# Channel attention followed by a top-128 expert layer: pass 1 of a batch and pass 2 of the batch before it, interleaved chunk by chunk

## The chip, the cores and the metric

The kernel runs on one core of a Trainium2 chip. The metric is the device time of one execution in microseconds (us): 358.91 us is the median of three runs (358.47 to 360.29). The core has a matrix engine (PE, which loads weights on PEld), a vector engine (DVE), a scalar engine (ACT), GpSimd (POOL), and SyncE (SP). In this kernel POOL issues all loads and SP all plain stores; 16 DMA engines move them. Each engine's instructions stand in the order in which the program wrote them, and wait on semaphores where an input is not there yet.

## The reference

For each of B = 4 batches, q, k, v are 6208 x 256 (float32):

```
s = kn.T @ qn / tau            # 256 x 256; qn, kn: columns divided by their norm over N
a = softmax(s, last axis)
x = v @ a                      # 6208 x 256
scores = x @ w_gate            # 6208
top = the 128 rows of x with the highest scores
out = x;  out[top] += sigmoid(scores[top]) * (relu(x[top] @ w1) @ w2)
```

So no row of `x` can be formed before all of q and k of its batch have been read (pass 1), and the expert layer of a batch can't choose its 128 rows before all its scores are there (after pass 2).

## The kernel before, in words

N is cut into six chunks of 1024 rows (8 rows to a partition) and a rest of 64. A chunk of q, k or v is one load by POOL that casts float32 to bf16: 1 MiB read, 512 KiB written to SBUF, a *tile* in what follows. The list `units` fixes the load order, and `pump` issues from it as long as the next entry has a free buffer (five chunk pairs of q and k, six chunks of v). `consumed(u)` frees the buffer of a unit at the place in the program where it was last used, and pumps; so the loads stand on POOL in that order, among the gathers and scatters.

- **Pass 1** (`p1_steps`, L187 to L191): per chunk eight steps of six matmuls, which add k.T q to `s_ps` and the Gram blocks (whose diagonals are the squared norms) to `g_ps`.
- **Softmax** (`softmax_a`, `softmax_b`, `softmax_c`, L204 to L264): mostly small DVE operations in a chain, one matmul (L233) that spreads a row of factors over the partitions, two exponentials on ACT. It leaves `a_sb` and, for the scores, `aw_sb` = a @ w_gate.
- **Pass 2** (`p2_groups`): a group is four rows to a partition, so a chunk has two. Eight PE transposes of v (L283), a DVE copy (L286), then for each row the output matmul (L309) and the score matmul (L312), both with the same transposed v as weights; ACT copies the output to a stage tile (L316), and SP stores a chunk of 1 MiB.
- **Expert layer** (`moe_stages`, a generator): seven rounds of counting (`cmp`, `cnt`, then a matmul at L367 that adds the counts over the partitions) close in on the score threshold; then the 128 row numbers (L414), a gather of their v rows (`vg`, POOL, L416), x again for these rows (L423 to L434), the two dense layers (L456, L464), and a scatter (POOL, L471). Each `yield` ends a stage. `slot()` lets the oldest generator run one stage; it is called between pieces of the passes, so a stage's instructions stand between those pieces on PE and DVE.

Before, the driver ran, for each batch, all of pass 1 with a slot at every second step, then the softmax, then all of pass 2; the expert layer of a batch ran in the slots of the next batch's pass 1, and that of the last batch by itself at the end:

```python
units = [(kind, b, ci) for b in range(B) for kind in ("qk", "v") for ci in range(NFULL + 1)]
...
for b in range(B):
    run_p1(b)
    ...
    run_p2(b)
    side.append(moe_stages(b))
```

The stores of batch 2 from chunk 1 on were held back (`deferred`) until the last but one load of all.

Of the kernel before, what the change touches and what calls it, by code (L numbers as in the profile page):

```python
# [9 lines left out]
F32 = mybir.dt.float32  # L10
# [16 lines left out]
def kernel(  # L27
# [30 lines left out]
    ST_BUFS = 12  # L58
# [5 lines left out]
    vt_pool = ctx.enter_context(tc.tile_pool(name="vt_pool", bufs=3))  # L64
# [24 lines left out]
    units = [(kind, b, ci) for b in range(B) for kind in ("qk", "v") for ci in range(NFULL + 1)]  # L89
# [65 lines left out]
    nc.vector.memset(wrow[:, NCOL - 1:NCOL], 0.0)  # L155
    ones_col = const.tile([P, NCOL], BF16)
# [15 lines left out]
    def p1_steps(b, ci):  # L172

        if ci == 0:
            acc[b] = (ps_s.tile([P, 2, C], F32, name="s_ps"), ps_g.tile([P, 4, P], F32, name="g_ps"))
# [23 lines left out]
    def softmax_a(b):  # L199
        s_ps, g_ps = acc[b]  # L200
        junk = smx.tile([P, P], F32, name="junk")
# [28 lines left out]
        for cc in range(2):  # L230
            nc.vector.tensor_scalar_mul(diag[:, cc, :], ident_f, rn[:, cc:cc + 1])
        rq_ps = ps_m.tile([P, 512], F32, name="m_ps")
        nc.tensor.matmul(rq_ps[:, 0:C], lhsT=ones_f, rhs=diag.rearrange("p a c -> p (a c)"),  # L233
                         start=True, stop=True)
        return rn, rq_ps

    def softmax_b(b, rn, rq_ps):
        s_ps, g_ps = acc[b]
# [4 lines left out]
        for cc in range(2):  # L243
            ss = smx.tile([P, C], F32, name=f"ss{cc}")
            nc.vector.scalar_tensor_tensor(out=ss, in0=s_ps[:, cc, :], scalar=rn[:, 2 + cc:3 + cc],  # L245
                                           in1=rq, op0=ALU.mult, op1=ALU.mult)
            nc.scalar.activation(e[:, cc, :], ss, AF.Exp, accum_out=rsum[:, cc:cc + 1])  # L247
        return e, rsum

    def softmax_c(b, e, rsum):  # L250
# [19 lines left out]
    deferred = []  # L270

# [17 lines left out]
    def p2_matmul(b, g, vt_sb):  # L289
        ci, s0, n = g  # L290
        parts = P if ci < NFULL else REM
        a_sb, aw_sb = a_tiles[b]
        if ci == 0 and s0 == 0:
            sc_tiles[b] = ps_sc.tile([P, NCOL, 2], F32, name="sc_ps")
        sc_ps = sc_tiles[b]
        if s0 == 0:
# [5 lines left out]
        for pair in range((n + 1) // 2):  # L302
            o_ps = ps_o.tile([P, 2, C], F32, name="o_ps")
            m = min(2, n - pair * 2)
            for pj in range(m):
                j = pair * 2 + pj
                col = ci * RPP + s0 + j
                for cc in range(2):
# [3 lines left out]
                    nc.tensor.matmul(sc_ps[:parts, col, :], lhsT=vt_sb[:, cc, j, :parts],  # L312
                                     rhs=aw_sb[:, cc, :],
                                     start=cc == 0 and col in (0, NCOL - 1),
                                     stop=cc == 1 and col >= NCOL - 2)
# [9 lines left out]
    def moe_stages(b):  # L325
# [8 lines left out]
        nc.vector.tensor_reduce(out=mx, in_=sc, axis=AX.X, op=ALU.max)  # L334
        yield
        mps = ps_m.tile([P, 512], F32, name="m_ps")
        nc.tensor.transpose(mps[0:1, 0:P], in_=mx, identity=ident_f)

        lohi = moe.tile([1, 2], F32, name="lohi")
        top = moe.tile([1, 1], F32, name="top")  # L340
        nc.vector.tensor_reduce(out=lohi[:, 0:1], in_=mps[0:1, 0:P], axis=AX.X, op=ALU.min)
        nc.vector.tensor_reduce(out=top, in_=mps[0:1, 0:P], axis=AX.X, op=ALU.max)
        nc.vector.tensor_tensor(out=lohi[:, 1:2], in0=top, in1=lohi[:, 0:1], op=ALU.subtract)
        yield
        mps = ps_m.tile([P, 512], F32, name="m_ps")
        nc.tensor.matmul(mps[:, 0:2], lhsT=ones_f[0:1, :], rhs=lohi, start=True, stop=True)
        steps = moe.tile([P, NSTEP], F32, name="steps")
        lo = moe.tile([P, NSTEP + 1], F32, name="lo")
        nc.vector.scalar_tensor_tensor(out=lo[:, 0:1], in0=mps[:, 1:2], scalar=-1e-6, in1=iota_col,
                                       op0=ALU.mult, op1=ALU.bypass)  # L350
        nc.vector.tensor_tensor(out=lo[:, 0:1], in0=mps[:, 0:1], in1=lo[:, 0:1], op=ALU.add)
        for i in range(NSTEP):
            nc.vector.tensor_scalar(out=steps[:, i:i + 1], in0=mps[:, 1:2],
                                    scalar1=1.00001 / (NTHR + 1) ** (i + 1), scalar2=None, op0=ALU.mult)
        for i in range(NSTEP):
# [113 lines left out]
        while deferred and b == B - 2:  # L469
            yield  # L470
# [105 lines left out]
```

## Time and profile before

| | |
|---|---|
| median of three runs | 358.91 us (358.47 to 360.29) |
| the profiled execution's own time | 358.95 us |
| its span, first to last instruction | 357.2 us |
| busy: PE, DVE, ACT, POOL | 220.6, 143.9, 65.8, 56.2 us |
| mean granted TensorE clock | 0.794 of 2.4 GHz |
| DMA: loads (queue q0), stores (queue q1) | 39.98 MB and 25.56 MB, as written |

The 1.75 us between span and time lie outside the instructions. The granted clock is that of PE: 1.0 means 2.4 GHz and 0.5 means 1.2 GHz. Loads count by the bf16 bytes that they write, half of what they read.

### The profile page before, as it was taken

The numbers are of one execution on the slowest core, as the hardware profiler recorded it, in microseconds if no ns is written. First come the engines' busy times: TensorE is split into PE (matmuls) and PEld (weight loads), VectorE is DVE, ScalarE is ACT, GpSimd is POOL, SyncE is SP. The second block draws the span as 40 slices with busy tenths as digits, with TensorE's granted clock in tenths as the row PEclk, the third lists the DMA queues.
The fourth block names the chain that finished last, engine by engine and source line by source line (L and its number), as shares of the span: only waits on it lengthen the run. The fifth ranks groups of instructions, "written<-read, shape, count | busy, mean of one in ns | idle before, by whom it ended". The sixth has DMA issues, their size and how long they took to land.

```text
span 357.2 us, 6052 instructions
## 1 busy us (share of the span) xinstructions
PE 220.6 (62%) x2528; PEld 189.5 (53%) x2528; DVE 143.9 (40%) x543; ACT 65.8 (18%) x129; POOL 56.2 (16%) x103
## 2 busy tenths in 40 slices
PE   0986546995670483898672854997686639930050
PEld 0775434984460382697562753896575628920030
DVE  0000054437820126444880246345862363458520
ACT  1000003660000011474000101671000115720010
POOL 7222322003132030000603030003310010000100
PEclk9999675999785595699888695799788957985555
DMA  7999999999999989187999967201998802850000
GB/s 133 213 213 210 212 212 213 277 317 314 291 213 212 212 155 206 64 345 309 178 214 210 215 135 144 119 2 26 212 213 290 347 15 117 352 246 0 2 6 15
DMA packets 17354, 65.91 MB, mean 185 GB/s; under 512 B 1968, under 2 KB 4656, under 8 KB 14256
## 3 DMA queue, kind: packets, MB, share of 16 engines
q0 software_dynamic: 13408, 39.98, 57.1%
q1 hardware_dynamic: 3920, 25.56, 17.4%
q8 instruction: 19, 0.31, 0.3%
q14 instruction: 7, 0.06, 0.0%
HBM read 79.04 MB, written 25.95 MB: 294 GB/s over the span
## 4 chain that ended last, share of the span: by engine, by line
issue 39%; DMA 29%; PE 19%; DVE 8%; POOL 2%; POOLq 0%; ACT 0%; ACTq 0%
DMA k_ch<-in_k_dram 13%; DMA v_ch<-in_v_dram 7%; PE s_ps L187 5%; DMA q_ch<-in_q_dram 5%; DMA vg<-in_v_dram,idx 4%; PE o_ps L309 4%; PE g_ps L191 3%; PE g_ps L189 3%; PE vt_ps L283 2%; DVE cmp L360 1%; DVE cnt L364 1%; POOL q_ch L105 1%; DVE junk L204 1%; DVE thr L357 1%; PE m_ps L233 1%
## 5 line engine op out<-in xcount | busy, mean ns | idle before, releaser
L187 PE MATMUL s_ps<-q_ch,k_ch 128*128 128x256 bf16 x384 | 103.4, 304 | 19.1 <-DMA k_ch<-in_k_dram 19.1
L189 PE MATMUL g_ps<-q_ch 128*128 128x128 bf16 x384 | 92.0, 240 | 0.0
L191 PE MATMUL g_ps<-k_ch 128*128 128x128 bf16 x384 | 91.7, 239 | 0.0
L309 PE MATMUL o_ps<-a_sb,vt_sb 128*128 128x256 bf16 x392 | 67.2, 287 | 10.8 <-DVE a_sb L258 10.2
L187 PEld LDWEIGHTS <-k_ch 128*128 128x128 bf16 x384 | 41.6, 108 | 38.2 <-DMA k_ch<-in_k_dram 19.6
L312 PE MATMUL sc_ps<-aw_sb,vt_sb 128*128 128x2 bf16 x392 | 58.6, 171 | 4.8 <-DVE aw_sb L264 4.8
L316 ACT COPY stage<-o_ps 128x512 f32<-128x512 f32 x96 | 54.3, 586 | 36.9 <-PE o_ps L309 36.8
L286 DVE COPY vt_sb<-vt_ps 128x1024 bf16<-128x1024 bf16 (+1 forms) x52 | 34.0, 655 | 55.6 <-PE vt_ps L283 55.6
L309 PEld LDWEIGHTS <-vt_sb 128*128 128x128 bf16 x392 | 40.9, 104 | 22.1 <-DVE a_sb L258 8.5
L191 PEld LDWEIGHTS <-k_ch 128*128 128x128 bf16 x384 | 42.0, 109 | 8.8
L189 PEld LDWEIGHTS <-q_ch 128*128 128x128 bf16 x384 | 41.5, 108 | 0.3
L312 PEld LDWEIGHTS <-vt_sb 128*128 128x128 bf16 x392 | 38.5, 98 | 2.9 <-issue 2.5
L283 PE MATMUL vt_ps<-ident_b,v_ch 128*128 128x128 bf16 x384 | 34.1, 244 | 0.0
L105 POOL DMA_DIRECT2D q_ch<-in_q_dram x24 | 13.4, 560 | 108.6 <-PE g_ps L191 96.5
L283 PEld LDWEIGHTS <-v_ch 128*128 128x128 bf16 x384 | 27.4, 111 | 2.3 <-issue 1.1
L446 ACT ACTIVATE gate<-ssc 128x1 f32<-128x1 f32 x4 | 0.8, 203 | 147.0 <-DVE ssc L443 147.0
L367 PE MATMUL m_ps<-cnt,ones_b 128*128 128x8 bf16 x28 | 4.7, 168 | 34.0 <-DVE cnt L364 34.0
L204 DVE CUSTOM_DVE_ANT_0 junk<-g_ps,ident_f 128x128 f32<-128x128 f32 x16 | 4.7, 291 | 49.7 <-PE g_ps L191 49.3
L423 PE MATMUL vt_ps<-ident_b,vg 128*128 128x128 bf16 x8 | 1.5, 282 | 32.9 <-DMA vg<-in_v_dram,idx 32.9
L247 ACT ACTIVATE e<-ss 128x256 f32<-128x256 f32 x8 | 3.3, 408 | 92.6 <-DVE ss L245 92.6
L423 PEld LDWEIGHTS <-vg 128*128 128x128 bf16 x8 | 0.5, 108 | 33.5 <-DMA vg<-in_v_dram,idx 33.5
L105 POOL DMA_DIRECT2D v_ch<-in_v_dram x24 | 13.0, 560 | 31.5 <-DMA k_ch<-in_k_dram 14.1
(116 smaller groups left out, 202.6 us busy)
## 6 DMA issues: line engine op xcount, KB each, us to landing
out_dram<-stage SPq DMA_DIRECT2D x24, 1024.0 KB, 5.6
q_ch<-in_q_dram POOLq DMA_DIRECT2D x24, 512.0 KB, 15.2
k_ch<-in_k_dram POOLq DMA_DIRECT2D x24, 512.0 KB, 15.4
v_ch<-in_v_dram POOLq DMA_DIRECT2D x24, 512.0 KB, 14.8
w_sb<-in_moe_w_dram POOLq DMA_DIRECT2D x2, 512.0 KB, 20.1
out_dram<-stage_rem SPq DMA_DIRECT2D x4, 64.0 KB, 8.3
wg_bcast<-in_moe_w_gate_dram SPq DMA_DIRECT2D x1, 128.0 KB, 3.8
q_rem<-in_q_dram POOLq DMA_DIRECT2D x4, 32.0 KB, 12.0
```

Of the source, the lines that this page charges most:

```text
L105: ins = nc.gpsimd.dma_start(out=t, in_=view(src, b, ci))
L187: nc.tensor.matmul(s_ps[:, cc, :], lhsT=ks[:, sl], rhs=qs, start=first and cc == 0, stop=last and cc == 1)
L189: nc.tensor.matmul(g_ps[:, cc, :], lhsT=qs[:, sl], rhs=qs[:, sl], start=first and cc == 0, stop=False)
L191: nc.tensor.matmul(g_ps[:, 2 + cc, :], lhsT=ks[:, sl], rhs=ks[:, sl], start=False, stop=last and cc == 1)
L204: nc.vector.tensor_tensor_reduce(out=junk, in0=g_ps[:, i, :], in1=ident_f, scale=1.0, scalar=0.0, op0=ALU.mult, op1=ALU.add, accum_out=nsq ...
L233: nc.tensor.matmul(rq_ps[:, 0:C], lhsT=ones_f, rhs=diag.rearrange("p a c -> p (a c)"), start=True, stop=True)
L283: nc.tensor.transpose(vt_ps[:, cc, j, :parts], in_=vt[:parts, s0 + j, cc * P:(cc + 1) * P], identity=ident_b[:parts, :parts])
L286: nc.vector.tensor_copy(vt_sb[:, :, :n, :parts], vt_ps[:, :, :n, :parts])
L309: nc.tensor.matmul(o_ps[:parts, pj, :], lhsT=vt_sb[:, cc, j, :parts], rhs=a_sb[:, cc, :], start=pj == 0 and cc == 0, stop=pj == m - 1 and ...
L312: nc.tensor.matmul(sc_ps[:parts, col, :], lhsT=vt_sb[:, cc, j, :parts], rhs=aw_sb[:, cc, :], start=cc == 0 and col in (0, NCOL - 1), stop= ...
L316: nc.scalar.copy(st[:parts, s0 + pair * 2:s0 + pair * 2 + m, :], o_ps[:parts, :m, :])
L367: nc.tensor.matmul(mps[:, 0:NTHR], lhsT=ones_b, rhs=cnt, start=True, stop=True)
```

## The change

- Load order and program order are now those of `phase(b)`: after the first chunk of q and k of batch b, two chunks of v of batch b-1 follow each chunk pair of q and k, until v is used up. Pass 2 of batch b-1 so runs between the chunks of pass 1 of batch b. There are B+1 phases; the last has v of the last batch alone.
- The softmax becomes a generator in three stages; it copies `s_ps` to SBUF first, so that the next pass 1 can take the PSUM bank. Slots come after each half chunk of pass 1 and each group of pass 2.
- Transposes of v are written two pieces ahead of their group.
- In the last batch, pass 2 first does only the scores (`p2_score`) for all groups, and keeps the 13 transposed groups (14 `vt` buffers in place of 3); then `moe_stages` of that batch starts, with one group of output matmuls (`p2_out`) after each of its stages.
- Held stores: batch 2 from chunk 2 on, behind the load of chunk 4 of the last v. Stage buffers go from 12 to 9.
- In the threshold search the range is found with one matmul in place of a transpose and a matmul, and the next thresholds are computed from the count directly, and no longer from the new lower bound `lo`.

The core of the diff:

```diff
-    units = [(kind, b, ci) for b in range(B) for kind in ("qk", "v") for ci in range(NFULL + 1)]
+    def phase(b):
+        if b == 0:
+            return [("qk", 0, ci) for ci in range(NFULL + 1)]
+        if b == B:
+            return [("v", B - 1, ci) for ci in range(NFULL + 1)]
+        items = []
+        nv = 0
+        for ci in range(NFULL + 1):
+            items.append(("qk", b, ci))
+            if ci >= 1:
+                for _ in range(2 if ci < NFULL // 2 + 1 else NFULL + 1):
+                    if nv <= NFULL:
+                        items.append(("v", b - 1, nv))
+                        nv += 1
+        return items
+    units = [u for b in range(B + 1) for u in phase(b)]
...
-    def softmax_a(b):
+    def softmax_stages(b):
         s_ps, g_ps = acc[b]
+        s_sb = smx.tile([P, 2, C], F32, name="s_sb")
+        nc.scalar.copy(s_sb, s_ps)
...
         for i in range(NSTEP):
...
+            if i + 1 < NSTEP:
+                base = moe.tile([P, NTHR], F32, name="base", bufs=2)
+                nc.vector.tensor_scalar(out=base, in0=iota_row[:, 1:NTHR + 1], scalar1=steps[:, i + 1:i + 2],
+                                        scalar2=lo[:, i:i + 1], op0=ALU.mult, op1=ALU.add)
             yield
...
+            if i + 1 < NSTEP:
+                thr = moe.tile([P, NTHR], F32, name="thr", bufs=2)
+                nc.vector.scalar_tensor_tensor(out=thr, in0=kk.to_broadcast([P, NTHR]),
+                                               scalar=steps[:, i:i + 1], in1=base, op0=ALU.mult,
+                                               op1=ALU.add)
             nc.vector.tensor_scalar(out=lo[:, i + 1:i + 2], in0=kk, scalar1=steps[:, i:i + 1],
                                     scalar2=lo[:, i:i + 1], op0=ALU.mult, op1=ALU.add)
...
+    def slot():
+        advance(smx_side)
+        advance(side)
...
+    def transposes(i, ahead):
+        while tq and tpos[tq[0]] <= i + ahead:
+            _, b, g = tq.pop(0)
+            vts[(b, g)] = p2_transpose(b, g)
+            if g[1] == 4 or g[0] == NFULL:
+                consumed(("v", b, g[0]))
+    last_groups = []
+    for i, a in enumerate(atoms):
+        if a[0] == "p1":
+            _, b, ci, lo_, hi_ = a
+            pump()
+            st = p1_steps(b, ci)
+            for f in st[lo_:hi_]:
+                f()
+            if hi_ != 4:
+                consumed(("qk", b, ci))
+        elif a[0] == "smx":
+            smx_side.append(softmax_stages(a[1]))
+            advance(smx_side)
+        else:
+            _, b, g = a
+            if b == B - 1:
+                transposes(i, 2)
+                while b not in a_tiles:
+                    advance(smx_side)
+                p2_score(b, g, vts[(b, g)], list(range(g[2])))
+                last_groups.append(g)
+                slot()
+            else:
+                while b not in a_tiles:
+                    advance(smx_side)
+                p2_out(b, g, vts.pop((b, g)), True)
...
+                if g[0] == NFULL:
+                    side.append(moe_stages(b))
+        transposes(i, 2)
+        slot()
+    side.append(moe_stages(B - 1))
+    flush_deferred()
+    for g in last_groups:
+        advance(side)
+        p2_out(B - 1, g, vts.pop((B - 1, g)), False)
```

Three places show what moves. The first is POOL's queue around the first gather (`vg`) of the expert layer. Before, it stands behind the loads of v of batch 1 and one chunk pair of batch 2, and what follows it are further chunk pairs of q and k:

```order
L108 DMA q_rem<-in_q_dram 64x256
L108 DMA k_rem<-in_k_dram 64x256
L105 DMA v_ch<-in_v_dram 128x2048 x6
L108 DMA v_rem<-in_v_dram 64x256
L105 DMA q_ch<-in_q_dram 128x2048
L105 DMA k_ch<-in_k_dram 128x2048
L416 DMA vg<-in_v_dram,idx 128x256
L105 DMA q_ch<-in_q_dram 128x2048
```

Now the gather of batch 0 stands behind the last loads of phase 2, the rest of q and k of batch 2 and the first chunk pair of batch 3:

```order
L124 DMA v_ch<-in_v_dram 128x2048 x2
L124 DMA q_ch<-in_q_dram 128x2048
L124 DMA k_ch<-in_k_dram 128x2048
L127 DMA v_rem<-in_v_dram 64x256
L124 DMA q_ch<-in_q_dram 128x2048
L124 DMA k_ch<-in_k_dram 128x2048
L127 DMA q_rem<-in_q_dram 64x256
L127 DMA k_rem<-in_k_dram 64x256
L124 DMA q_ch<-in_q_dram 128x2048
L124 DMA k_ch<-in_k_dram 128x2048
L455 DMA vg<-in_v_dram,idx 128x256
L124 DMA q_ch<-in_q_dram 128x2048
```

The gather moved from behind one chunk pair of the batch whose pass 1 is running to behind all of that batch's loads.

The second place is PE at the end of pass 1 of batch 1, where the softmax begins (`m_ps<-diag`), now; `cnt` are the counts of the threshold search of batch 0:

```order
L214 LDWEIGHTS k_rem
L214 MATMUL g_ps<-k_rem 128x128
L401 LDWEIGHTS ones_b
L401 MATMUL m_ps<-cnt,ones_b 128x8
L259 MATMUL m_ps<-diag,ones_f 128x256
L401 LDWEIGHTS ones_b
L401 MATMUL m_ps<-cnt,ones_b 128x8
L210 LDWEIGHTS k_ch
L210 MATMUL s_ps<-q_ch,k_ch 128x256
```

Before, `m_ps<-diag` followed the last step of pass 1 at once, and transposes of v came behind it; now a round of the threshold search stands on either side of it, and pass 1 of the next batch behind both.

The third place is PE in the expert layer of the last batch, at the threshold search. Before, its rounds follow one another:

```order
L346 MATMUL m_ps<-lohi,ones_f 128x2
L367 LDWEIGHTS ones_b
L367 MATMUL m_ps<-cnt,ones_b 128x8
L367 LDWEIGHTS ones_b
L367 MATMUL m_ps<-cnt,ones_b 128x8
```

Now eight output matmuls stand between one round and the next (here the last two of one such group and the first of the next):

```order
L343 LDWEIGHTS vt_sb
L343 MATMUL o_ps<-a_sb,vt_sb 128x256
L343 LDWEIGHTS vt_sb
L343 MATMUL o_ps<-a_sb,vt_sb 128x256
L401 LDWEIGHTS ones_b
L401 MATMUL m_ps<-cnt,ones_b 128x8
L343 LDWEIGHTS vt_sb
L343 MATMUL o_ps<-a_sb,vt_sb 128x256
```

The output matmuls of the last batch moved from ahead of its expert layer to between its stages.

## Rows read from the trace of the kernel before

**Rows 1.** The page's part 2: DMA busy tenths in 40 slices of the span.

```profile
DMA  7999999999999989187999967201998802850000
```

**Rows 2.** Windows: stretch, length, busy time (instructions) by engine, clock, DMA share, GB/s.

```profile
20.00:30.00 10.00, 7.07 (x94) 6.39 (x93) 0.00 (x0) 0.00 (x0) 2.15 (x4) 1.00 1.06 212
121.00:137.00 16.00, 11.69 (x132) 10.45 (x132) 5.89 (x31) 1.29 (x3) 3.15 (x5) 0.82 0.92 181
228.00:242.00 14.00, 14.00 (x219) 12.91 (x218) 6.11 (x11) 10.44 (x19) 0.00 (x0) 1.00 0.18 76
315.00:348.00 33.00, 7.16 (x42) 4.16 (x42) 19.87 (x83) 1.60 (x4) 1.26 (x2) 0.59 0.11 41
```

**Rows 3.** DMA queues from 70 to 90 us: packets, MB, share of 16 engines.

```profile
q0 software_dynamic: 575, 2.09, 51.6%
q1 hardware_dynamic: 572, 4.16, 51.6%
```

**Rows 4.** Chain that ended last: start, us, what.

```profile
20.08 19.91 DMA k_ch<-in_k_dram
...
224.24 0.88 PE vt_ps L283 x8
...
228.67 0.47 PE vt_ps L283 x8
...
239.31 0.47 PE vt_ps L283 x8
...
266.09 5.24 DMA vg<-in_v_dram,idx
```

**Rows 5.** Timeline of PE, end of pass 1 of batch 3: start, us, what.

```profile
280.99 0.27 PE L187 MATMUL s_ps<-q_ch,k_ch 128*128 128x256 bf16 x1
...
282.10 0.27 PE L187 MATMUL s_ps<-q_ch,k_ch 128*128 128x256 bf16 x1
```

**Rows 6.** Timeline of POOL: start, us, what, idle before and its releaser.

```profile
30.19 0.54 POOL L105 DMA_DIRECT2D v_ch<-in_v_dram  x1 [1.92 <-DMA k_ch<-in_k_dram]
...
106.79 1.03 POOL L416 DMA_INDIRECT vg<-in_v_dram,idx  x1 [2.27 <-DMA v_ch<-in_v_dram]
...
129.65 1.01 POOL L471 DMA_INDIRECT out_dram<-upd,idx  x1 [12.81 <-DVE upd L467]
...
169.09 0.53 POOL L105 DMA_DIRECT2D q_ch<-in_q_dram  x1 [35.41 <-PE g_ps L191]
```

**Rows 7.** Timeline of PE at the gather of batch 0.

```profile
121.24 0.40 PE L423 MATMUL vt_ps<-ident_b,vg 128*128 128x128 bf16 x2 [16.69 <-DMA vg<-in_v_dram,idx]
```

**Rows 8.** Timeline from the softmax of batch 3 to its second dense layer.

```profile
283.06 0.29 DVE L204 CUSTOM_DVE_ANT_0 junk<-g_ps,ident_f 128x128 f32<-128x128 f32 x1 [3.59 <-PE g_ps L191]
...
287.72 1.22 PE L233 MATMUL m_ps<-diag,ones_f 128*128 128x256 f32 x2 [4.70 <-DVE diag L231]
...
294.82 0.16 PE L312 MATMUL sc_ps<-aw_sb,vt_sb 128*128 128x2 bf16 x1 [1.20 <-DVE aw_sb L264]
...
314.88 0.26 DVE L330 TENSOR_REDUCE sc<-sc_ps 128x48 f32<-128x96 f32 x1 [1.53 <-PE sc_ps L312]
...
318.56 0.56 DVE L364 TENSOR_REDUCE cnt<-cmp 128x8 bf16<-128x392 bf16 x1
...
320.84 0.56 DVE L364 TENSOR_REDUCE cnt<-cmp 128x8 bf16<-128x392 bf16 x1
...
332.97 0.17 DVE L370 TENSOR_SCALAR_CACHE_REDUCE ge<-m_ps 128x8 f32<-128x8 f32 x1 [0.26 <-PE m_ps L367]
...
336.66 0.15 DVE L414 TENSOR_SCALAR idx<-fl 128x1 int32<-128x1 f32 x1
...
340.34 0.40 PE L423 MATMUL vt_ps<-ident_b,vg 128*128 128x128 bf16 x2 [4.84 <-DMA vg<-in_v_dram,idx]
...
345.14 1.76 PE L464 MATMUL o_ps<-w_sb,h_sb 128*128 128x256 bf16 x8
```

**Rows 9.** The page's part 5: groups, busy us, mean ns of one, idle before.

```profile
L286 DVE COPY vt_sb<-vt_ps 128x1024 bf16<-128x1024 bf16 (+1 forms) x52 | 34.0, 655 | 55.6 <-PE vt_ps L283 55.6
```

More of the change, by code (lines that the diff above doesn't have):

```diff
@@ L155 @@
     nc.vector.memset(wrow[:, NCOL - 1:NCOL], 0.0)
+    pows = const.tile([P, NSTEP], F32)
+    for i in range(NSTEP):
+        nc.vector.memset(pows[:, i:i + 1], 1.00001 / (NTHR + 1) ** (i + 1))
     ones_col = const.tile([P, NCOL], BF16)
@@ L270 @@
     deferred = []
+    gate_done = []
+    held = {b: NFULL + 1 for b in range(B)}
+    side = []
     def p2_groups(b):
@@ L342, in moe_stages @@
[L342 to L346, printed above, removed]
+        nc.tensor.matmul(mps[:, 0:P], lhsT=ones_f, rhs=dmx, start=True, stop=True)
+        lo = moe.tile([P, NSTEP + 1], F32, name="lo")
+        top = moe.tile([P, 1], F32, name="top")
@@ L347, in moe_stages @@
         steps = moe.tile([P, NSTEP], F32, name="steps")
[L348 to L351, printed above, removed]
+        nc.vector.tensor_scalar(out=steps, in0=pows, scalar1=rng, scalar2=None, op0=ALU.mult)
+        thr = moe.tile([P, NTHR], F32, name="thr", bufs=2)
@@ L468, in moe_stages @@
                                        op1=ALU.add)
-        while deferred and b == B - 2:
+        while held[b] or (b >= B - 2 and deferred):
             yield
@@ L482, in flush_deferred @@
             st = emit_store(*deferred.pop(0))
-            if first:
+            if not gate_done:
+                gate_done.append(1)
                 tc.add_manual_dep(
-                    st.ins, load_inst[units[-2]].ins.name,
+                    st.ins, load_inst[units[-3]].ins.name,
                     mybir.DependencyInfo(mybir.DependencyClass.Sync, mybir.DependencyReason.DATA),
-                    reason="stores behind the last load")
-            first = False
-    def slot():
-        while side:
-            try:
-                next(side[0])
-                return
-            except StopIteration:
-                side.pop(0)
@@ L498, in run_p1 @@
-    def run_p1(b):
-        for ci in range(NFULL + 1):
+                    reason="stores behind the last loads")
+            n -= 1
+    atoms = []
+    for b in range(B + 1):
+        for kind, bb, ci in phase(b):
+            if kind == "qk":
+                if ci < NFULL:
+                    atoms += [("p1", bb, ci, 0, 4), ("p1", bb, ci, 4, 8)]
+                else:
+                    atoms.append(("p1", bb, ci, 0, 1))
+                    atoms.append(("smx", bb))
+            else:
+                n = 4 if ci < NFULL else 1
+                for s0 in ((0, 4) if ci < NFULL else (0,)):
+                    atoms.append(("p2", bb, (ci, s0, n)))
```

128 lines of the change are left out of this document (63 added, 65 removed).

## The prediction

> **What bounds the kernel now.** I read the DMA row of the slices first. Ten of its 40 digits are 0, 1 or 2 [rows 1]; a slice is 357.2/40 = 8.93 us, so for some 89 us the DMA engines do next to nothing. Between these holes they are saturated: loads alone move 212 GB/s at a share above 1 [rows 2]. The holes are therefore what can be won. POOL's timeline says where they come from: at 169.09 us it had waited 35.41 us for pass 1 of PE to free a q buffer [rows 6]. The load order has all of v behind all of q and k, so during a pass 2 the next chunk pairs have no buffer, and pass 2 frees only v buffers that the list can't use yet. The last hole is the expert layer of batch 3, alone from 315 us on, DMA share 0.11 and PE 7.16 us busy in 33 [rows 2].
>
> Two prices of DMA. A tile (512 KiB) at 212 GB/s is 2.47 us. Where loads and stores run together, both queues hold 51.6% of the engines; in those 20 us the 2.09 MB of loads are 4.0 tiles, 9.8 us at the price above, so the 4.16 MB of stores (3.97 chunks) took the other 10.2 us, 2.57 us a chunk [rows 3]. Two prices of PE at full clock: a chunk of pass 1 is 16 half steps of (282.10-280.99)/5 = 0.222 us, 3.55 us [rows 5]; a group of pass 2 with its transposes is (239.31-228.67)/7 = 1.52 us [rows 4], where the clock was 1.00 [rows 2].
>
> **The new order, up to the end of pass 1 of batch 3.** One repeating unit (a chunk pair of q and k, two chunks of v, two stores) costs DMA 4x2.47 + 2x2.57 = 15.0 us and PE 3.55 + 4x1.52 = 9.6 us. So the loads set the pace, POOL stands at a load that waits for an earlier landing, as it did at 30.19 us (1.92 us for a k tile) [rows 6], and everything behind that place in POOL's queue waits too. That hits the gather. It stood behind one chunk pair of the running batch and still came late: issued at 106.79, its transposes had waited 16.69 us when they began at 121.24 [rows 6, 7]. Now it stands behind the rest of that batch's loads and one chunk pair of the next, while PE needs it right after the transposes of chunk 2 of v. Everything on PE is queued behind it, with the DVE copies, stores and freed buffers that follow.
>
> When does it land? The k tile of the 14th load landed at 20.08+19.91 = 40.0 us [rows 4], and up to there nothing is moved. From there to the first gather stand 12+6+12+6+2 = 38 tiles and six rests of 1/16, 38.4x2.47 = 94.8 us, and eight stores, 20.6 us. With 2.5 us for the gather itself (an estimate, below the 3.5 us that it took on an idle queue with its issue, from `idx` at 336.66+0.15 to PE at 340.34 [rows 8]) that is G0 = 158 us. PE ends pass 1 of batch 1 at 40.0 + 18.4x2.47 + 6x2.57 + 3.5 = 104, and, by the stretch worked out below, is at the gather 33 us later, at 137; it waits 21 us. The loads lose almost nothing by this: four tiles stand free behind the gather (9.9 us).
>
> From G0 on PE has landed data and is itself the chain:
> - Gather to scatter took 129.65-121.24 = 8.4 us [rows 6, 7] with five double steps (0.89 us each) between; four groups in their place make it 10.0.
> - One chunk of pass 1, four groups, a chunk, the rest of v, a chunk and the rest, with 1.5 us of waits for counts: 3.55+6.1+3.55+0.5+3.55+1.5 = 18.8. Pass 1 of batch 2 ends at 187.
> - Softmax. Before, it held PE from 283.06 to 294.82 [rows 8], 11.8 us. Its first DVE part now stands behind a round of the threshold search, and PE has only the count ahead of `diag`: 1.4 until the count, a round of 2.28 (320.84-318.56), 4.7 to `diag` (287.72-283.06) and its 1.22 us matmul [rows 8], 9.6 us with little PE work.
> - Four more rounds, 9.1, and 3.5 of softmax's later part on DVE, which hide two chunks of pass 1; row numbers 3.84 (332.97 to 336.81 [rows 8]), which hide two groups; then two groups and a chunk, 6.6. PE reaches the second gather 9.6+9.1+3.5+3.8+6.6 = 32.6 us after the end of pass 1: G1 = 219.5.
>
> The DMA bound says about the same by another way: 56.7 tiles from 40.0 us to the second gather, 140 us, and 14 stores, 36 us, give 218.5. So a shorter chain on PE would win no more than a microsecond there. Behind G1: again 10.0 and 18.8, end of pass 1 of batch 3 at 248. Some of this runs at 1.2 GHz after waits: where PE resumed after the 16.69 us wait, the granted clock of the next 16 us was 0.82 [rows 2]. For the restarts behind the gathers and the softmaxes I take 5 us in all, bounds 0 and 20: **253 us**, before 283.06, so 30 us earlier.
>
> The Trainium skill, page TensorE: Matmul & The Clock Gate, section HAM oscillation, says that matmul bursts separated by waits for DMA each start again at half clock. By that rule all of phase 1 would run at 1.2 GHz; its three units would then cost PE 19.2 us each in place of DMA's 15.0, PE would reach the first gather at 150 in place of 137, still ahead of 158, and the sum would stay. The 0.82 above agrees with the rule.
>
> **The last batch.** Softmax and scores, now with the rest of batch 2's expert layer in the same in-order queues. Six rounds of the search 13.7; softmax 11.8 between them on DVE; two copies of v.T in its way 1.3 (0.66 each [rows 9]); row numbers 3.8; gather 3.5; then to the second dense layer 345.14-340.34 = 4.8 [rows 8] and 1.8 for a group in between (eight transposes at low clock are 0.88 [rows 4], eight scores about the same), and 1.8 for that layer; three groups and the rest of scores 5.3. Sum 48. Before, softmax and pass 2 took 314.88-283.06 = 31.8 [rows 8]: the scores without outputs save little, the search in between costs more, 16 us lost. End of scores: 301.
>
> From scores to the end of the span it was 357.2-314.88 = 42.3. The `lo` leaves the path: 0.2 in each of six rounds and 0.4 in the range, -1.6 (bounds 0 and -2.5). Outputs between the rounds: eight matmuls, at most 1.7 us at 1.2 GHz, within the 1.9 us in which PE waits for a count; take +0.5. The gather beside stores took 5.24 [rows 4] against 3.5: +1.8. Sum 43, so the span ends at 344, and with the 1.75 us outside it the profiled execution (358.95, within 0.1 of the median) becomes **346 us**.
>
> Priced at nothing: the copy of `s_ps` (ACT, beside 1.3 us of DVE work on `g_ps` that the next pass 1 awaits anyway); the constants `pows` (DVE, before the first tile has landed); fewer stage buffers (a batch needs nine only if stores lag by a batch; without that cover a group waits a store's 2.57); the held stores, 4.06 chunks, 10.4 us in the scores, where DMA has only 15 us of v; POOL's scatter of batch 2, which waits for them.
>
> **Rivals.**
> - *PE stays slow* (slower). Between 158 and 253 us PE has 22 groups and nine chunks, 66 us at full clock. My sum lets 5 us of it run at 1.2 GHz. From 18 us on, a bit over a quarter, the gain is gone; with 25 us the time is 366. For it: the 0.82 after a wait, and more waits on DVE between short pieces than before. Against: 1.00 where pieces follow one another [rows 2]. Chance 0.14.
> - *The last batch costs less* (faster). If the search of batch 2 is ahead of my place by its slots, the rounds are done before softmax, and 48 becomes 38: 336. Against: the order has six of the seven counts behind pass 1. Also here: the low clock costs nothing, 341. Chance 0.16.
> - *The scatter blocks the loads* (no change). POOL waited 12.81 us at it [rows 6]; now 14 tiles of load stand between it and the next gather. My cover is the four tiles behind the gather; if the scatter comes 23 us after the gather, not 10, both G1 and the end move by 13: 359. Chance 0.08.
>
> **The numbers.** My sum holds 0.62 of the chance with its own range of 338 to 356. About 0.5% is what a measurement of this kernel can tell from no change, 357.1 to 360.7. Faster is the sum and the second rival, 0.78; same is the third, 0.08; slower the first, 0.14. The range of 334 to 363 leaves one in ten on either side: at the low end clock and last batch both come cheap, at the high end 22 us of work run at low clock.
>
> **What would show it.** Right: DMA busy with no slice near 0 from the start until about 215 us; a wait of some 20 us of PE for `vg` near 140 to 158, a short or no one near 220; softmax waits of PE near 10 us in batches 1 and 2; pass 1 of batch 3 over near 253, its scores near 301, threshold rounds of about 2.1 us beside output matmuls, and stores spread over the tail. Wrong: a `vg` wait that starts before 125 or ends after 170 (my count of tiles or prices), DMA holes between 160 and 215 (the scatter or PE), a granted clock below 0.7 between 160 and 250, or over 55 us from the end of pass 1 to the end of scores.

## The result, and the profile of the changed kernel

The changed kernel takes **342.16 us** (median of four runs, 341.71 to 343.50) against 359.38 us (358.47 to 360.29): ratio **0.9527**, 95% interval 0.9488 to 0.9566. The profiled execution took 343.5 us with a span of 341.4.

DMA busy tenths of the changed kernel, to be laid beside [rows 1] (a slice is now 8.54 us):

```profile
DMA  7999999999999999999879999943594000046800
```

The first hole of [rows 1] (the digit 1) is gone, the second (2, 0, 1) now reads 4, 3, 5; DMA is busy without a gap for 26 slices, to 222 us, forecast to about 215. The empty stretch near the end is still there, but it now lies ahead of the last stores, not behind them.

Windows of the changed kernel, columns as in [rows 2]; the cuts lie at the first gather's use, around the softmax of batch 2, around PE's wait for the second gather, at the end of pass 1 of batch 3 and at the end of the scores:

```profile
158.00:190.00 32.00, 27.96 (x363) 24.82 (x358) 12.15 (x41) 11.03 (x21) 6.88 (x12) 0.93 0.92 244
190.00:204.00 14.00, 7.37 (x52) 5.79 (x53) 11.57 (x54) 0.91 (x4) 0.00 (x0) 0.55 1.06 217
204.00:219.00 15.00, 14.33 (x208) 13.20 (x208) 9.96 (x40) 4.49 (x8) 4.26 (x7) 1.00 1.04 221
219.00:226.00 7.00, 0.64 (x11) 0.47 (x9) 0.69 (x1) 0.00 (x0) 0.56 (x1) 0.79 0.98 269
226.00:256.00 30.00, 27.80 (x361) 24.84 (x360) 10.04 (x31) 10.51 (x20) 3.15 (x5) 0.93 0.57 154
256.00:297.00 41.00, 19.14 (x232) 16.04 (x230) 30.67 (x120) 2.89 (x8) 2.01 (x2) 0.58 0.11 42
297.00:341.00 44.00, 20.29 (x149) 13.74 (x149) 19.80 (x86) 14.82 (x28) 1.96 (x2) 0.75 0.37 149
```

From 158 to 190 and from 226 to 256 PE is busy for 28 of 32 and 30 us at a clock of 0.93: there PE is the chain, as the prediction had it. From 256 on DVE is busy for 31 of 41 us, with PE at 19.

Timelines of PE and of POOL at the first two gathers, and of PE at the softmax of batch 2 (columns as in [rows 5, 6]):

```profile
157.18 0.39 PE L462 MATMUL vt_ps<-ident_b,vg 128*128 128x128 bf16 x2 [18.08 <-DMA vg<-in_v_dram,idx]
...
195.88 0.79 PE L259 MATMUL m_ps<-diag,ones_f 128*128 128x256 f32 x1 [6.49 <-DVE diag L256]
...
225.82 0.39 PE L462 MATMUL vt_ps<-ident_b,vg 128*128 128x128 bf16 x2 [6.36 <-DMA vg<-in_v_dram,idx]
...
146.63 1.02 POOL L455 DMA_INDIRECT vg<-in_v_dram,idx  x1 [4.58 <-DMA k_ch<-in_k_dram]
...
214.50 1.01 POOL L455 DMA_INDIRECT vg<-in_v_dram,idx  x1 [1.35 <-DVE idx L453]
```

PE has the first gather at 157.18 (forecast 158). The second is issued when its row numbers are there (`idx`), and PE still has it only 225.82-214.50 = 11.3 us later.

What PE waited for, in the whole span (us, times, longest); `vg` are the gathered rows, `k_ch` a chunk of k, `diag` the factors of the softmax, `cnt` the counts of the threshold search:

```profile
PE vt_ps L462 <- DMA vg<-in_v_dram,idx: 31.8, 4, 18.1
PE s_ps L210 <- DMA k_ch<-in_k_dram: 25.4, 6, 9.7
PE m_ps L259 <- DVE diag L256: 24.2, 4, 6.5
PE m_ps L401 <- DVE cnt L393: 18.9, 18, 2.2
```

In the kernel before, the same view gives:

```profile
PE m_ps L367 <- DVE cnt L364: 34.0, 28, 2.3
PE vt_ps L423 <- DMA vg<-in_v_dram,idx: 32.9, 4, 16.7
PE s_ps L187 <- DMA k_ch<-in_k_dram: 19.1, 4, 9.8
PE m_ps L233 <- DVE diag L231: 18.8, 4, 4.7
PE o_ps L309 <- DVE a_sb L258: 10.2, 4, 2.6
```

So the sum of the waits for gathers hardly changed (32.9 to 31.8 us). The waits for counts fell by 15.1 and those for `a_sb`, 10.2, are gone from the list; waits for `k_ch` (+6.3) and `diag` (+5.4) take 11.7 back. What of the change brought this, the experiments were to tell.

### The profile page after: what moved, and what is told of

Its sections match the earlier page's. It is cut to its first block, busy times and chain, and to the rows that moved or that the text cites. A ratio compares the mean times of both kernels' runs of the same rounds, so it can differ in the third digit from the quotient of the medians.

```text
span 341.4 us, 6038 instructions
## 1 busy us (share of the span) xinstructions
PE 216.0 (63%) x2524; PEld 186.0 (54%) x2524; DVE 139.9 (41%) x550; ACT 67.3 (20%) x133; POOL 56.0 (16%) x103
## 4 chain that ended last, share of the span: by engine, by line
DMA 37%; issue 26%; PE 18%; DVE 11%; POOL 3%; ACT 1%; POOLq 1%; SPq 0%; DVEq 0%; ACTq 0%
DMA k_ch<-in_k_dram 27%; DMA v_ch<-in_v_dram 5%; DMA vg<-in_v_dram,idx 4%; PE o_ps L343 4%; PE s_ps L210 4%; PE vt_ps L306 3%; DVE cnt L393 2%; PE g_ps L214 2%; PE g_ps L212 2%; DVE cmp L389 2%; DMA out_dram<-stage_rem 1%; ACT stage L348 1%; PE o_ps L503 1%; POOL q_ch L124 1%; PE m_ps L259 1%
## 5 line engine op out<-in xcount | busy, mean ns | idle before, releaser
L210 PE MATMUL s_ps<-q_ch,k_ch 128*128 128x256 bf16 x384 | 100.6, 299 | 25.6 <-DMA k_ch<-in_k_dram 25.4
L212 PE MATMUL g_ps<-q_ch 128*128 128x128 bf16 x384 | 90.6, 236 | 0.0
L214 PE MATMUL g_ps<-k_ch 128*128 128x128 bf16 x384 | 90.5, 236 | 0.0
L343 PE MATMUL o_ps<-a_sb,vt_sb 128*128 128x256 bf16 x392 | 60.8, 283 | 1.7 <-ACT stage L348 0.6
L309 DVE COPY vt_sb<-vt_ps 128x1024 bf16<-128x1024 bf16 (+1 forms) x52 | 33.9, 654 | 64.2 <-PE vt_ps L306 63.3
L210 PEld LDWEIGHTS <-k_ch 128*128 128x128 bf16 x384 | 41.1, 107 | 30.9 <-DMA k_ch<-in_k_dram 26.4
L214 PEld LDWEIGHTS <-k_ch 128*128 128x128 bf16 x384 | 41.2, 107 | 8.0
L212 PEld LDWEIGHTS <-q_ch 128*128 128x128 bf16 x384 | 41.1, 107 | 0.3 <-issue 0.3
L322 PEld LDWEIGHTS <-vt_sb 128*128 128x128 bf16 x392 | 34.1, 102 | 9.9 <-issue 4.8
L343 PEld LDWEIGHTS <-vt_sb 128*128 128x128 bf16 x392 | 29.0, 99 | 13.7 <-issue 11.6
L322 PE MATMUL sc_ps<-aw_sb,vt_sb 128*128 128x2 bf16 x392 | 33.2, 167 | 4.8 <-DVE aw_sb L284 4.6
L306 PEld LDWEIGHTS <-v_ch 128*128 128x128 bf16 x384 | 26.1, 107 | 6.2 <-issue 5.9
L124 POOL DMA_DIRECT2D q_ch<-in_q_dram x24 | 13.5, 562 | 59.1 <-PE g_ps L214 30.1
L462 PE MATMUL vt_ps<-ident_b,vg 128*128 128x128 bf16 x8 | 1.6, 300 | 31.8 <-DMA vg<-in_v_dram,idx 31.8
L124 POOL DMA_DIRECT2D v_ch<-in_v_dram x24 | 12.8, 538 | 52.3 <-PE vt_ps L306 15.6
L259 PE MATMUL m_ps<-diag,ones_f 128*128 128x256 f32 x8 | 4.9, 713 | 24.2 <-DVE diag L256 24.2
L124 POOL DMA_DIRECT2D k_ch<-in_k_dram x24 | 13.1, 546 | 31.1 <-DMA k_ch<-in_k_dram 11.5
L401 PE MATMUL m_ps<-cnt,ones_b 128*128 128x8 bf16 x28 | 4.7, 168 | 20.8 <-DVE cnt L393 18.9
## 6 DMA issues: line engine op xcount, KB each, us to landing
q_ch<-in_q_dram POOLq DMA_DIRECT2D x24, 512.0 KB, 17.5
k_ch<-in_k_dram POOLq DMA_DIRECT2D x24, 512.0 KB, 18.8
v_ch<-in_v_dram POOLq DMA_DIRECT2D x24, 512.0 KB, 15.1
q_rem<-in_q_dram POOLq DMA_DIRECT2D x4, 32.0 KB, 19.1
```

Source lines behind the costliest of these rows:

```text
L124: ins = nc.gpsimd.dma_start(out=t, in_=view(src, b, ci))
L210: nc.tensor.matmul(s_ps[:, cc, :], lhsT=ks[:, sl], rhs=qs, start=first and cc == 0, stop=last and cc == 1)
L212: nc.tensor.matmul(g_ps[:, cc, :], lhsT=qs[:, sl], rhs=qs[:, sl], start=first and cc == 0, stop=False)
L214: nc.tensor.matmul(g_ps[:, 2 + cc, :], lhsT=ks[:, sl], rhs=ks[:, sl], start=False, stop=last and cc == 1)
L306: nc.tensor.transpose(vt_ps[:, cc, j, :parts], in_=vt[:parts, s0 + j, cc * P:(cc + 1) * P], identity=ident_b[:parts, :parts])
L309: nc.vector.tensor_copy(vt_sb[:, :, :n, :parts], vt_ps[:, :, :n, :parts])
```

## The experiments

The tables and ratios below give medians; "softmax 3" is the start of the first softmax operation of batch 3 on DVE (`junk<-g_ps`), "scores" the start of the reduction of its scores (`sc<-sc_ps`). In the changed kernel these are 260.1 and 297.6 us.

**Later use of the gather**, in batches 0 and 1:

```diff
-        for _ in range(4):
+        for _ in range(4 if b >= B - 2 else 10):
             yield
```

> The expert layer of batches 0 and 1 uses its gathered rows ten slots after the gather, not four. Theory A (the DMA limits the way to the second gather, so a wait of PE for a gather mostly costs what DMA would have cost anyway): the two waits of 18.1 and 6.4 us go, but PE then waits for tiles in their place; the last tile of pass 1 of batch 3 can't land before 40 + 54.7x2.47 + 14x2.57 = 211 us, so pass 1 of batch 3 ends between 232 and 250 (256 now) and the time is 322 to 336. Theory B (the waits are hidden wholly, PE is not the chain): 340 to 343. Theory C (the gather's place in the queue is the whole cost): 24.5 us less, 318.

Measured: 329.92 us, ratio to the kernel before 0.9181 (0.9143 to 0.9218); softmax 3 at 246.6. PE's waits for `vg` fell from 31.8 to 20.5 us in all. The time is in theory A's range, but the waits for tiles that it expected did not come (`k_ch` 25.1 us, 25.4 without the edit). The waits for a gather before the last batch are on the path: 11.3 us of them go, and 12 us come back for six slots.

**Outputs of the last batch with its scores**, as in the batches before it:

```diff
-                p2_score(b, g, vts[(b, g)], list(range(g[2])))
-                last_groups.append(g)
+                p2_out(b, g, vts.pop((b, g)), True)
...
+                    emit_store(b, g[0])
```

> The last batch computes outputs and scores together again, and its expert layer runs alone at the end. Theory A (scores first pays because PE and ACT work of 13 groups leaves the way to the scores): 13 groups of eight matmuls, 0.85 us at full clock and 1.7 at half, of which PE's waits in that stretch can hide about half: scores 5 to 12 us later, and the end without outputs beside it 2 us shorter: 345 to 352. Theory B (the way to the scores is the chain on DVE of softmax and search, outputs fit in PE's waits): 340 to 343.

Measured: 346.81 us (0.9656, 0.9605 to 0.9707). Scores at 304.2, 6.6 later, and 40.4 us behind them in place of 43.8. Scores first is worth 4.7 us.

**The old load order in the changed kernel:**

```diff
     def phase(b):
-        items = []
-        nv = 0
...
-        return items
+        return ([("v", b - 1, ci) for ci in range(NFULL + 1)]
+                + [("qk", b, ci) for ci in range(NFULL + 1)])
```

> Loads and passes in the old order (all of v of batch b-1, then all of q and k of batch b), all else as changed. Theory A (interleaving buys the earlier end of pass 1 of batch 3, and loses some of it because the search of batch 2 moves into the last batch): pass 1 of batch 3 ends at 278 to 290, from there to the end 26 us to the scores and 44 behind, in all 350 to 360. Theory B (the gain comes from the last batch and the search, interleaving is worth nothing): 340 to 346.

Measured: **332.74 us** (0.9275, 0.9241 to 0.9310): without the interleaving the changed kernel is 9.4 us *faster*, which neither theory had. Softmax 3 is at 261.7, only 1.6 later than with it, and scores are 23.6 us behind that in place of 37.5. Windows of this kernel, pass 1 of batch 1, then pass 2, pass 1 of batch 2:

```profile
79.00:106.00 27.00, 24.64 (x324) 22.19 (x321) 17.58 (x75) 1.01 (x3) 6.96 (x13) 1.00 1.05 284
106.00:162.00 56.00, 24.65 (x317) 20.98 (x316) 17.77 (x62) 15.74 (x32) 6.32 (x10) 0.70 0.87 222
162.00:187.00 25.00, 24.11 (x318) 21.79 (x316) 17.42 (x74) 0.62 (x2) 8.57 (x16) 1.00 0.97 211
```

In the kernel before, the same pass 1 of batch 1 was

```profile
80.00:133.00 53.00, 29.06 (x315) 25.17 (x311) 19.50 (x81) 1.29 (x3) 12.63 (x22) 0.77 1.02 235
```

27 us at a clock of 1.00 against 53 at 0.77. The load order is the same; what differs in pass 1 is above all the pace of slots, one for four steps in place of two. The pace also moves the gather's use out of pass 1. The new search stands there too; a run further down changes the pace alone.

**The old threshold search:**

```diff
-        nc.tensor.matmul(mps[:, 0:P], lhsT=ones_f, rhs=dmx, start=True, stop=True)
+        nc.tensor.transpose(mps[0:1, 0:P], in_=mx, identity=ident_f)
...
-                nc.vector.scalar_tensor_tensor(out=thr, in0=kk.to_broadcast([P, NTHR]),
```

> The threshold search as before (range by transpose and matmul, thresholds from the lower bound), all else as changed. A round took 1.95 us where it was 2.28. Theory A (13 rounds lie on the path, seven at the end and six ahead of the last scores): 13x0.33 + 0.5 = 4.8 us more, 347. Theory B (only the seven at the end count): 2.8 more, 345. Theory C (rounds are set by what stands between them): 342.

Measured: 342.36 us (0.9526, 0.9478 to 0.9573), the changed kernel's time. From scores to the end it is 45.9 us in place of 43.8, near the 1.6 that the prediction gave the search, but softmax 3 came 5 us earlier and scores 2.6. The new search is worth nothing in sum. Why softmax 3 came earlier was not tried; with the old search PE waited 4.0 us less for gathers and 5.3 more for counts.

**All of v in one block** behind the second chunk of q and k:

```diff
-                for _ in range(2 if ci < NFULL // 2 + 1 else NFULL + 1):
+                for _ in range(NFULL + 1):
```

> All chunks of v of the preceding batch are loaded and used in one block behind the second chunk of q and k, where the changed kernel has two chunks of v behind each; nothing else is changed. Theory G (the loss of the changed kernel against its own kernel in the old load order sits in the last batch, where the threshold search of batch 2 shares the queues with the softmax and scores of batch 3): pass 2 of batch 2 ends earlier, its search runs in the slots of pass 1 of batch 3, so the time from the softmax's first DVE instruction of batch 3 to the end of its scores falls from 37.5 us to about 24 us; the time is 322 to 332 us. Rival H (the loss comes from the alternation of v and q, k loads as such, or from the gathers' place behind loads): the stretch stays at 33 us or more, or the end of pass 1 comes as much later; 338 to 346 us.

Measured: 322.28 us (0.8960, 0.8904 to 0.9016). Softmax 3 at 249.6, scores at

```profile
276.27 0.26 DVE L362 TENSOR_REDUCE sc<-sc_ps 128x48 f32<-128x96 f32 x1 [0.46 <-PE sc_ps L322]
```

26.7 us behind it: theory G, whose range the time just meets. Half of the 20 us lies there, the other half ahead of softmax 3, which G did not say.

**The kernel before, at half the pace of slots**, nothing else:

```diff
-                if s % 2 == 1:
+                if s % 4 == 3:
                     slot()
```

> The kernel before, with one stage of the expert layer for every fourth step of pass 1 in place of every second; order of loads, softmax, search and last batch are those of before. Theory S (the old order is faster in the changed driver because the stages come at half the pace, so that PE does not stand at the count matmuls and at the gather's use inside pass 1): the 16.7 us wait for the gather of batch 0 leaves pass 1, the softmax of batch 1 begins near 106 to 115 us in place of 133, that of batch 3 near 262 to 270 in place of 283, and the time is 338 to 347 us. Rival R (the pace of the stages is worth nothing; the staged softmax, the scores ahead of the outputs and the deeper buffers bring it): 355 to 361 us, softmax of batch 3 near 280.

Measured: **331.85 us** (four runs from 327.50 to 333.99, too far apart for an interval; the kernel before took 359.90, and the pages and views here are those of the run of 330.50). One number in the old kernel gains 26 to 32 us, more than the whole change. Softmax 3 is at 250.0. Windows of pass 1, pass 2, pass 1 of batches 1 and 2:

```profile
79.00:106.00 27.00, 23.51 (x303) 20.97 (x300) 17.55 (x76) 0.02 (x1) 6.95 (x13) 1.00 1.05 283
106.00:158.00 52.00, 26.90 (x326) 23.12 (x326) 17.66 (x58) 15.48 (x31) 6.34 (x10) 0.74 0.93 236
158.00:185.00 27.00, 23.85 (x308) 21.39 (x306) 17.63 (x75) 0.51 (x2) 9.11 (x17) 1.00 0.98 217
```

Pass 1 runs at full clock; the wait for the gather (16.0 us) has moved into pass 2.

**Later use of the gather combined with the old load order, and with v in one block** (the diffs are those above):

> The changed kernel in the old load order (all v of the preceding batch, then all q and k), and the use of the gathered rows of batches 0 and 1 put off by six more slots. Theory L (every wait of PE for a gather before the last batch is lost time, as in the interleaved order, where the same edit brought 12 us): the two waits of 23.8 and 16.6 us fall to under 3 us each, and the time from 332.7 to 313 to 323 us. Rival M (in this order PE waits there for what it would wait for anyway, the loads of the next chunks): the waits move to the chunk loads and the time stays at 329 to 335 us.

> All v in one block behind the second chunk of q and k, and the use of the gathered rows of batches 0 and 1 put off by six more slots: both edits at once. If theory G and the gain of 12 us by the late use add up, 310 to 322 us, the fastest of all so far. If they overlap (the block has its gather waits hidden already), within 4 us of the block alone. If rival H holds, 326 to 333 us, the late use alone.

Measured: 320.48 us (0.8897, 0.8846 to 0.8948) and **312.86 us** (0.8673, 0.8622 to 0.8724), the fastest of all. The first time lies in the range of theory L, though the two waits fell only to 16.0 and 5.9 us. In the second the two edits nearly add up (12.2 and 19.9 us apart, 29.3 together). Of 25.5 us of waits for gathers the longest is one of 17.5 us (PE at the gather, and POOL's issue of it):

```profile
149.10 0.39 PE L462 MATMUL vt_ps<-ident_b,vg 128*128 128x128 bf16 x2 [17.47 <-DMA vg<-in_v_dram,idx]
...
126.31 1.03 POOL L455 DMA_INDIRECT vg<-in_v_dram,idx  x1 [2.27 <-DVE vt_sb L309]
```

**The old pace in the changed kernel**, with the new and with the old load order:

```diff
-            for f in st[lo_:hi_]:
+            for n_, f in enumerate(st[lo_:hi_]):
                 f()
+                if n_ == 1:
+                    slot()
```

> The changed kernel with one more slot in the middle of each half chunk of pass 1, so that a batch's stages come at about the pace of the kernel before (38 slots a batch in place of 26); nothing else is changed. Theory S (the pace is what the changed kernel gained by): the count matmuls and the use of the gather stand closer together and earlier, PE waits longer for counts (19 us now) and for the first gather (18 us now), the softmax of batch 3 begins at 270 us or later (260 now); the last batch gives up to 10 us back, since the search of batch 2 is over before its softmax; time 347 to 360 us. Rival I (the order of loads and passes is what it gained by): softmax of batch 3 within 4 us of 260, and with the shorter last batch 332 to 342 us.

> The changed kernel in the old load order and with the old pace of stages: what is left of the change is the staged softmax, the transposes written ahead, the new search and the scores ahead of the outputs in the last batch. Theory S (pace alone brought the kernel in the old order from 359 to 333 us): pass 1 of batches 1 to 3 takes over 40 us each again, at a granted clock below 0.9, the softmax of batch 3 begins at 275 us or later (262 with the slow pace), and the time is 345 to 358 us; what it stays below 359 by is the worth of the scores ahead of the outputs, some 8 us. Rival P (the pace matters only in the old driver, the staged softmax is what brings it): 329 to 337 us.

Measured: 345.87 us (0.9612, 0.9577 to 0.9647) and 361.36 us (1.0054, 1.0029 to 1.0078). The first fits neither theory: at this pace the interleaved kernel loses only 3.7 us (softmax 3 at 266.9, 33 us to the scores). The second is theory S, and slower still than its range: pass 1 of batch 2 takes 51 us again, and the 8 us given to the scores ahead of the outputs don't show in the sum.

**The kernel before, gather used later**, at the old pace. The use then stands at the same place among PE's instructions as at half the pace:

```diff
-        for _ in range(4):
+        for _ in range(4 if b == B - 1 else 16):
             yield
```

> The kernel before, old pace of stages, with 16 slots between the issue of a gather and its use in batches 0 to 2 in place of 4: the use then stands at the very place among PE's instructions where the half pace put it, in pass 2, while the threshold search stays at the old pace in pass 1. Theory W (the half pace gained by taking the gather's use out of pass 1): all of its 27 us come back, and since the gather is issued earlier than at half pace it is waited for less: softmax of batch 3 at 245 to 255 us, 320 to 333 us. Theory C (it gained by spacing the count matmuls, and with them the clock in pass 1): the softmax of batch 1 begins at 112 us or later, count waits of 34 us stay, and the time is 338 to 350 us.

Measured: **327.87 us** (0.9106, 0.9041 to 0.9171), softmax 3 at 248.7, both as theory W had them. Two of the waits of PE, the row of PE at the first gather (it has no wait), and the DMA row:

```profile
PE m_ps L367 <- DVE cnt L364: 33.9, 28, 2.3
...
PE vt_ps L423 <- DMA vg<-in_v_dram,idx: 4.9, 1, 4.9
```

```profile
131.79 0.27 PE L423 MATMUL vt_ps<-ident_b,vg 128*128 128x128 bf16 x2
```

```profile
DMA  7999999999999999999999998009989536720000
```

The waits for counts stay at 34 us, those for the gather fall by 28.0, PE's busy time by 220.6-215.6 = 5.0; together 33.0, and the span is 30.6 shorter. Pass 1 of batch 1 now takes 34 us (78.2 to 112.1) in place of 53. The first hole of [rows 1] is gone too, with the same buffers and the same load order; the second is not (the digits 0, 0 at 204 to 220 us).

**The kernel before, with more loads ahead:**

```diff
-    QK_BUFS = 5
+    QK_BUFS = 8
...
-    ST_BUFS = 12
+    ST_BUFS = 9
```

> The kernel before with eight chunk pairs of q and k in SBUF in place of five (and nine stage tiles in place of twelve): POOL can load three pairs more during pass 2, 15 us of DMA work at 2.47 us a tile for each of three holes. Theory D (the holes in the DMA row are what can be won, as the prediction read it): the 35 us wait of POOL for a q buffer shrinks to about 15 us, and the time falls by 20 to 45 us, to 315 to 339 us. Theory N (pass 1 of the kernel before is not bound by its loads but by PE's waits inside it, so that a load that comes earlier is not worth anything): the holes move to another place, the time stays at 353 to 361 us.

Measured: **375.34 us** (1.0429, 1.0345 to 1.0512), slower than either theory had it. PE at the first gather, and POOL's issue of it:

```profile
136.31 0.40 PE L423 MATMUL vt_ps<-ident_b,vg 128*128 128x128 bf16 x2 [39.81 <-DMA vg<-in_v_dram,idx]
```

```profile
117.17 0.54 POOL L105 DMA_DIRECT2D k_ch<-in_k_dram  x1
119.56 1.01 POOL L416 DMA_INDIRECT vg<-in_v_dram,idx  x1 [1.86 <-DMA q_ch<-in_q_dram]
```

The gather stands on POOL behind the loads that the new buffers allow: it is issued 12.8 us later than before (119.56 for 106.79 [rows 6]), PE has it at 136.3 and waits 39.8 us for it, with pass 1 queued behind. Before it had been 121.2 and 16.7 [rows 7]. So this run doesn't price the holes alone: more loads ahead also delayed the gather, and more buffers together with a later use were not tried.

The eleven kernels that differ in order, pace and the gather's use, medians in us (the kernel before has 357.93 to 362.09 in all its runs; the 331.9 stands for 327.5 to 334.0):

| order | old pace | half pace | half pace, gather used later |
|---|---|---|---|
| old, driver of before | 359.4 | 331.9 | - (old pace, used later: 327.9) |
| old, changed driver | 361.4 | 332.7 | 320.5 |
| interleaved (the change) | 345.9 | 342.2 | 329.9 |
| v in one block | - | 322.3 | 312.9 |

And where the time of PE went in the corners of that table, from each page's part 1 and the view of PE's waits (us). Busy time and all waits together come to 10.8 to 11.9 us less than the span in each of them, so what differs between two kernels is in these columns but for a few us:

| kernel | span | busy | `vg` | `cnt` | `diag` | `k_ch` |
|---|---|---|---|---|---|---|
| before | 357.2 | 220.6 | 32.9 | 34.0 | 18.8 | 19.1 |
| before, half pace | 328.8 | 209.5 | 23.1 | 21.9 | 21.1 | 19.4 |
| before, gather used later | 326.6 | 215.6 | 4.9 | 33.9 | 19.1 | 18.9 |
| changed driver, old order, old pace | 358.2 | 218.3 | 50.3 | 22.8 | 19.4 | 18.9 |
| changed driver, old order, half pace | 328.3 | 209.6 | 45.0 | 8.2 | 19.8 | 19.3 |
| interleaved, old pace | 343.8 | 218.6 | 24.6 | 23.0 | 24.1 | 27.4 |
| interleaved, half pace (after) | 341.4 | 216.0 | 31.8 | 18.9 | 24.2 | 25.4 |

## Why the prediction was right in time and wrong in part of the cause

- **First gather, pass 1 of batch 2.** Forecast 158 and 187. PE had the gather at 157.18; the last matmul of pass 1 ended at 188.0. The count of tiles and stores at 2.47 and 2.57 us holds (it has six rests where eight stand, 0.3 us). PE ended pass 1 of batch 1 at 107.6 (forecast 104) and was at the gather at 139.1 (forecast 137), so its wait was 18.1, forecast 21.
- **Softmax behind a round of the search.** Forecast 9.6 us from the end of pass 1 to the end of the `diag` matmul. Measured 188.0 to 195.88+1.22 = 197.1: 9.1.
- **Second gather.** PE was there at 225.82-6.36 = 219.46, forecast 219.5. But the "2.5 us for the gather itself" leaned on a gather on an idle queue; among loads it took 11.3. The term was too small by 8.8 us, 6.4 of which PE waited.
- **Low clock.** Forecast 5 us up to the end of pass 1 of batch 3, bounds 0 and 20. From the second gather to there it was 30.7 us (225.8 to 256.5), of which the sum had 28.8 at full clock, and behind the first gather 30.8 (157.2 to 188.0) for the same 28.8. All of the excess stands between gather and scatter, 12.0 and 11.9 us for 10.0, at a granted clock of 0.82 and 0.83; the rest took 18.8 both times, as summed, at 1.00. So low clock is worth at most 2 us behind each gather. The 5 us were too much, and made up for half of the second gather's error: 256.5 against 253. The rival in which PE stays slow did not come: 0.93 in both long stretches. Nor did the rival of the scatter: POOL issued it 12.0 us behind the first gather's use, and no slice of DMA fell below 7 up to 222 us. In the first phase the granted clock was 0.86, from 47 to 111 us, so most of it ran at 2.4 GHz. The Trainium skill, page TensorE: Matmul & The Clock Gate, section HAM oscillation, has a burst of matmuls start again at half clock after a wait for DMA. The 0.82 and 0.83 agree with it; that a whole phase would run so was the prediction's own step, and the 0.86 doesn't show it.
- **End of pass 1 to the scores of batch 3.** Forecast 48, measured 297.6-256.5 = 41.1: over-sized by 7. The row numbers were there at 283.06, 26.6 us on, for which the sum had 13.7+11.8+1.3+3.8 = 30.6; the last groups and scores took the rest less. The rival of a cheaper last batch (38) came more than half way, but not for its reason: the scores of batch 2 came at 251.0 us, so the search did fall behind the softmax.
- **Scores to the end.** Forecast 43, measured 43.8.

The errors, +3.5, -6.9 and +0.8, sum to -2.6: span 341.4, forecast 344. That the errors of the gather, the clock and the last batch cancel so nearly is luck.

**What failed lies in the cause.** First, the step "The holes are therefore what can be won", with loads that stand for want of a buffer. With the gather used later, and buffers and load order as they were, the kernel before is 32 us faster and the first hole is gone: there PE, standing at the gather in the middle of pass 1, was the bound. With buffers for three more pairs it is 15 us slower. The step is not wrong throughout: the second hole stays in the kernel with the later use, and v in one block, which leaves no hole until pass 1 of batch 3 ends, is 10.5 us faster than the old order at the same pace, and 7.6 with the later use. DMA rows of the old order and of v in one block, both in the changed driver at half pace:

```profile
DMA  7999999999999999936889999933059992056700
DMA  7999999999999999999797999999995000057700
```

That the filled holes bring this is not shown: the waits for gathers are shorter too (45.0 to 28.6 us in the first pair, 26.3 to 25.5 in the second).

The prediction read the wait for the first gather [rows 7] and carried it into the new order, but didn't ask what it cost in the old one.

Second, the pace of slots. The change halves it in pass 1, and the prediction gave that no price. In the old order the pace alone is worth some 28 us: waits for counts 12 to 15 us, busy time of PE 9 to 11 (the clock in pass 1 of batch 1 is 1.00 and no longer 0.77), waits for the gather 5 to 10. So theory W, right in its time, doesn't tell where the half pace gains: late use takes 28 us out of the gather's waits, half the pace takes most of its gain elsewhere. The old driver with both was not tried.

What the new order is worth so depends on the pace. At the old pace it brings 361.4-345.9 = 15.5 us, and the change with the old pace is 13.5 us faster than the kernel before, about the 13 that were forecast. But what falls are the waits for gathers, by 25.7, where the prediction had the first of them grow; those for `k_ch` and `diag` grow by 13.2. At the pace that the change has, it costs 342.16-332.74 = 9.4 us (13.1 between the two spans): the gathers fall by 13.2, but counts, busy time, `diag` and `k_ch` grow by 10.7+6.4+4.4+6.1 = 27.6. Part of this stands in the last batch. The scores of batch 2 end at 251.0 us (236.2 in the old order), so its search falls behind the softmax of batch 3 on DVE, and there are 37.5 us from softmax 3 to the scores in place of 23.6. PE's waits between 256 and 297 us in the changed kernel show the search (`cnt`) and the gather's use among those of the softmax:

```profile
PE m_ps L259 <- DVE diag L256: 6.5, 1, 6.5
PE m_ps L401 <- DVE cnt L393: 5.4, 4, 2.2
PE sc_ps L322 <- DVE aw_sb L284: 4.6, 1, 4.6
PE vt_ps L462 <- DMA vg<-in_v_dram,idx: 2.3, 1, 2.3
```

With v in one block those scores end at 230.3, the wait for counts there is gone, and the stretch is 26.7 us. So order and pace relieve some of the same waits, and their gains don't add up.

Open stays why the block also brings softmax 3 10.6 us sooner than the interleaving, and why the scores ahead of the outputs are worth 4.7 us in the interleaved kernel and nothing that shows in the old order at the old pace; there the waits for gathers are 17.4 us longer than before, which may hide it. Neither was tried apart.

## What to carry to other kernels

Where an engine waits for a transfer, ask what stands queued behind the wait. Before reordering loads, move the use of that transfer further from its issue: here one number (4 to 16 slots) was worth 32 us, nearly twice the whole change. When a change bundles an order with a pace, price each alone and both together; a profile with holes in DMA doesn't say that more prefetch fills them: here it delayed the gather and cost 15 us.

## What the runs showed of the hardware that was not expected

A gather that writes 64 KB can take as long as the 512 KiB loads issued around it. From its issue to the matmul that waited it was 2.8 us on an idle queue at the end of the kernel before (issued at 337.58, used at 340.34 [rows 8]), 10.6 and 11.3 us at the first two gathers of the changed kernel, 14.5 at the first of the kernel before [rows 6, 7], 16.7 with more buffers, and 22.8 in the fastest version, in a stretch without a pause of DMA (126.31 to 149.10). The loads themselves take about as long in the view of DMA issues of the old-order version:

```profile
v_ch<-in_v_dram POOLq DMA_DIRECT2D x24, 512.0 KB, 15.0
...
vg<-in_v_dram,idx POOLq DMA_INDIRECT x4, 11.7
```

The last column is the median from issue to landing (four gathers, 5.4 to 16.8 us). The size is the same in all of these, so what sets the time is what is in flight. With three more chunk pairs allowed ahead of it PE had the gather 15 us later (136.3 for 121.2), but only 2.3 us of this are its time in flight; 12.8 are its later issue by POOL.

The Trainium skill, page DMA: Bandwidth & Descriptors, section Anatomy of one DMA, fits a transfer issued from GpSimd as 2.0 us and its bytes at 436 GB/s, by which 64 KB would take some 2.2 us (an estimate from that page). The 2.8 us on the idle queue, up to the matmul, come near it; among loads the gathers above took 8 to 20 us more.
